# Two-pass attention and gated MLP on one core: another order of side work in slot one, in the pairs and at the end

## The chip, the core and the metric

One core of a Trainium2 chip runs the whole program. The metric is the device time of one launch in microseconds (us), the median of several runs. The engines are TensorE (PE, with its weight loads as PEld), VectorE (DVE), ScalarE (ACT), GpSimd (POOL) and SyncE (SP, which here only issues DMAs). Each runs its own list of instructions in order and waits where an input is not there yet.

## The reference

```python
def _attn_ref(q, k, v):              # (4, 12, 448, 64)
    scores = (1.0 / np.sqrt(q.shape[-1])) * np.matmul(q, k.transpose(0, 1, 3, 2))
    scores = np.where(mask, -1000000000.0, scores)      # causal
    attn = np.exp(scores - np.max(scores, axis=-1, keepdims=True))
    attn = attn / (np.sum(attn, axis=-1, keepdims=True) + 1e-09)
    return np.matmul(attn, v)

def _moe_ref(x, w_in, w_out):        # x: (1792, 768), w_in: (768, 2048), w_out: (2048, 768)
    h = x @ w_in
    g = h * np.cos(h)
    return g @ w_out
```

The attention's result, with its heads side by side, is `x`.

## The kernel before

**Numbers in halves.** Every large product is made from upper and lower halves: a value `t` is cast to a short float (`hi`), and `lo` is what is left, `t - hi`. A product is then three matmuls, hi·hi, hi·lo and lo·hi. A *half* below is one such operation: the upper one is a cast on ACT (lines 590, 681, 958), the lower one a subtraction, mostly on POOL (591, 682, 961), in two places on DVE.

**Attention** (to about 185 us) makes `x` for all 1792 rows and keeps it on the chip. The MLP then runs in two passes over the rows.

**Pass one** takes the first 1024 rows in two blocks of 512 and walks through `w_in` and `w_out` in eight groups; a block in a group is a *slot*, 16 in all. In a slot, PE makes two sums of `x @ w_in` (`m1_sum`, lines 564 to 566, 36 matmuls) and then four *chunks* of `g @ w_out` for the slot before (`m2a_chunk`, line 660, 12 matmuls of 384 columns each); DVE takes each chunk out of the banks into `acc` (lines 646, 648). Chunks use two pairs of banks in turn, so the third chunk waits for DVE's add of the first. Beside this, `cosine_stages` (572 on ACT, 574 on DVE, 576 and 577 on ACT, 579 on DVE) makes `g` from each sum, and the next group's weights are prepared: `mask_stages` (157, 159, 161 on ACT), `pack_stages` (three DVE passes 168, 172, 176), `halve` (681 and 682, then DMAs to DRAM), and sums of weights (`first_side`, `total`, line 700 on POOL; `side_out` then takes their halves). Slot 0 has only its chunks' inputs from the attention; slot 1 is the first that prepares weights, and for it the old code shares the order of all others, with `ia`, `ib` the weights packed in this slot and `ic` the next one's.

**Pass two** takes the other 768 rows with Strassen-like sums: for each pair of groups seven products `product(nx, n)` (line 1003, nine matmuls) of block sums of `w_in` and `x`, from which `g`'s four blocks a11, a12, a21, a22 come, and seven block products `blocks(g, n)` (line 1023, nine matmuls) with `w_out`. One iteration of the loop `for g in range(NG - 1)` is called a *pair* here: it has seven *steps* of one product for the next pair and one block product for this one. In between stand, in the code's order: the cosine's passes (`begin`, `go`, `end`), the sums s1 to s4 of blocks of `g` (`less`, line 954 on POOL) and their halves (`hi` line 958, `lo` line 961), and the four sums of raw `w_out` blocks for the next pair (`sub(nx, i)` with i = 4, 5, 3, 6, line 954; their halves `w_hi`, `w_lo`). The raw weights of a pair come with one DMA (`load_raw`, line 951) into one buffer, so its load waits for the last `sub` of the pair before:

```python
sub(nx, 4)
if g:
    a21 = end("21")
go("12")
w_hi(nx, 4)
go("12")
```

**The end.** Seven accumulators of block products are merged into four by sums on POOL and DVE (`merge`, line 1034, three operations each), the last group's products are added by PE (`m2_part`, line 1041) and DVE subtracts these (`m2_out`, line 1051) and stores the rows (line 1052). In the order of the queues nothing is scheduled by a planner: the instructions stand on each engine as the code is written.

Of the kernel before, what the change touches and what calls it, by code (L numbers as in the profile page):

```python
# [21 lines left out]
def kernel(  # L22
# [15 lines left out]
    nc = tc.nc  # L38
# [571 lines left out]
    def mask(i):  # L610
        if i < len(todo):
            for masks[i] in mask_stages(staged[i], i == 1):
                yield
# [18 lines left out]
    def moe(ring, early, firsts):  # L632
        pend = None
        with tc.tile_pool(name="mo", bufs=1) as mo:
# [219 lines left out]
            def slot(g, t0, n, k, prev, first):  # L854
# [6 lines left out]
                if k > 1:  # L861
                    mb = mask(ib)
                    some(mb, 2)
                else:
                    mb = opening[1]
# [99 lines left out]
            def sub(g, i):  # L965
                if g >= NG - 1:
                    return
                w11, w12, w21, w22 = raws[min(g, 1)]
                t = mo.tile([P, EH], F32, tag="tr", bufs=3, name="tr")
                if i == 4:  # L970
                    less(t, w12, w11)
                elif i == 5:
                    less(t, w22, sums_of.pop(4)[0])
                elif i == 3:
                    less(t, w21, sums_of[5, 0])
                else:
                    less(t, w22, w12)
                w = wouts[g, i]
                sums_of[i] = t, (w[:, 0], w[:, 1])
                if i == 5:  # L980
                    sums_of[5, 0] = t
                return
# [64 lines left out]
            def m2_out(j, c, o, rows):  # L1047
                i = (TA + j * TH) // P + c
                for e in range(2):
                    d = part(rows[e], c)  # L1050
                    nc.vector.tensor_tensor(d, d, o[:, e, 0:EH], op=ALU.subtract)
                    nc.sync.dma_start(
                        out=out[i * P : (i + 1) * P, e * EH : (e + 1) * EH], in_=d
                    )
# [46 lines left out]
            for g in range(NG - 1):  # L1101
# [8 lines left out]
                sub(nx, 4)  # L1110
# [3 lines left out]
                w_hi(nx, 4)  # L1114
# [7 lines left out]
                blocks(g, 0)  # L1122
                a12 = end("12")
# [5 lines left out]
                w_lo(nx, 4, nc.vector)  # L1129
# [4 lines left out]
                sub(nx, 5)  # L1134
                lo(g_ops[6], s3)
                lo(g_ops[1], a12)
                w_hi(nx, 5)
# [3 lines left out]
                blocks(g, 2)  # L1141
                s4 = less(sm0, a12, s2)
                sub(nx, 3)
                hi(g_ops[2], s4)
                lo(g_ops[2], s4)
                w_hi(nx, 3)
# [6 lines left out]
                begin("22", o)  # L1153
                blocks(g, 3)
                w_lo(nx, 3, nc.vector)
                go("22")
                go("22")
                sub(nx, 6)
                w_lo(nx, 5)
                w_hi(nx, 6)  # L1160
                if last:
                    merge(5, 0, nc.gpsimd)
                fetch_in(4)
                if g + 2 < NG - 1:
                    load_raw(g + 2)
# [3 lines left out]
                blocks(g, 4)  # L1169
                a22 = end("22")  # L1170
                go("11")
                go("11")
                hi(g_ops[3], a22)
                w_lo(nx, 6)
                lo(g_ops[3], a22)
                if last:
                    merge(6, 5, nc.gpsimd)
# [4 lines left out]
                blocks(g, 5)  # L1182
                a11 = end("11")
                go("21")
                go("21")
                hi(g_ops[0], a11)
                lo(g_ops[0], a11)
                fetch_in(6)
                if last:
                    blocks(g, 6)  # L1190
                    r = end("21")
                    hi(g_ops[6], r)
                    lo(g_ops[6], r)
# [6 lines left out]
            merge(3, 6, nc.gpsimd)  # L1200
# [3 lines left out]
            merge(4, 6, nc.vector, (0,))  # L1204
            r = end("12")
            merge(4, 6, nc.vector, (1, 2))
            hi(g_ops[1], r)
            lo(g_ops[1], r)
# [85 lines left out]
```

## Time and profile before

| | |
|---|---|
| time, median of 3 runs | 642.78 us (642.08 to 643.11) |
| the profiled execution | 640.33 us |
| its span | 638.6 us |
| PE busy | 621.9 us, 97% of the span |
| DVE, ACT, POOL busy | 487.3, 427.5, 429.6 us |

The span runs from the first to the last instruction of the profiled execution; its time also holds what lies around it. Busy time is the sum of an engine's instructions. PE at 97% still has idle places, and where the granted clock is under 1.00 it is busy at a lower speed. A list of waits says for each engine and line what it waited for: microseconds in total, times, and the longest. The chain of waits is followed back from the last instruction.

### The profile page before, as it was taken

What the parts mean: (1) busy time and instruction counts of PE and PEld (TensorE: products, weight loads), DVE (VectorE), ACT (ScalarE), POOL (GpSimd) and SP (SyncE); (2) the same over time, 40 slices, a digit from 0 to 9 for tenths busy, and PEclk for the clock granted to TensorE, in tenths of its full rate; (3) what the DMA queues carried; (4) which work ended last, traced back from release to release, by engine and by line L of the source; (5) the groups of instructions that cost most, each with busy time, mean ns of one, the idle gap of its engine ahead of it and who ended that gap; (6) DMA issues with size and microseconds to landing.
All of it is one profiled execution on the core that took longest, in us unless ns stands there. A gap on an engine that the chain in (4) does not pass through costs nothing.

```text
span 638.6 us, 11491 instructions
## 1 busy us (share of the span) xinstructions
PE 621.9 (97%) x3709; PEld 545.0 (85%) x3709; DVE 487.3 (76%) x1085; ACT 427.5 (67%) x953; POOL 429.6 (67%) x423
## 2 busy tenths in 40 slices
PE   8999999999998999999999999999979999999996
PEld 6667776766677999999999999999979999999995
DVE  5888888888737777887787777734349878888887
ACT  6989998998866777787777777732335444644540
POOL 3666656666626878777877787743385797679664
PEclk9999999999999999999999999999979999999999
DMA  5546556556505887869786978589956647558204
GB/s 124 138 115 148 145 119 159 142 131 162 156 10 199 251 314 240 312 201 341 231 314 198 350 244 311 195 326 393 410 193 241 232 136 276 206 204 280 54 1 149
DMA packets 124988, 133.29 MB, mean 209 GB/s; under 512 B 73056, under 2 KB 109264, under 8 KB 124928
## 3 DMA queue, kind: packets, MB, share of 16 engines
q1 hardware_dynamic: 118112, 107.31, 53.1%
q0 software_dynamic: 4928, 24.78, 10.4%
q10 hardware_dynamic: 1888, 0.46, 0.3%
q8 instruction: 30, 0.49, 0.3%
q14 instruction: 30, 0.25, 0.1%
HBM read 82.58 MB, written 49.94 MB: 208 GB/s over the span
## 4 chain that ended last, share of the span: by engine, by line
PE 86%; DVE 7%; ACT 3%; issue 2%; POOL 1%; DVEq 0%; ACTq 0%; POOLq 0%
PE banks L660 20%; PE banks L1023 12%; PE banks L1003 11%; PE banks L441 7%; PE banks L565 6%; PE banks L566 6%; PE banks L564 6%; PE banks L346 5%; PE banks L417 4%; PE banks L355 3%; PE banks L319 2%; DVE pb L363 2%; PE banks L924 1%; PE banks L427 1%; PE banks L1041 1%
## 5 line engine op out<-in xcount | busy, mean ns | idle before, releaser
L648 DVE TENSOR_TENSOR acc<-acc,banks 128x768 f32<-128x768 f32 (+1 forms) x122 | 111.9, 931 | 46.0 <-PE banks L660 36.9
L660 PE MATMUL banks<-w,gh 128*128 128x384 f32 x512 | 109.8, 335 | 2.7 <-DVE acc L646 2.7
L395 POOL TENSOR_TENSOR pb<-pb,stat 128x768 f32<-128x768 f32 (+2 forms) x72 | 73.9, 1040 | 41.8 <-ACT flat L329 19.9
L660 PEld LDWEIGHTS banks<-w,gh 128*128 128x128 f32 x512 | 90.8, 188 | 4.4 <-DVE acc L646 3.1
L377 ACT ACTIVATE pb<-pb,stat 128x384 f32<-128x384 f32 (+1 forms) x144 | 72.5, 512 | 15.9 <-DVE stat L363 15.9
L564 PE MATMUL banks<-xa,w 128*128 128x512 f32 x192 | 75.0, 391 | 0.0
L566 PE MATMUL banks<-xa,w 128*128 128x512 f32 x192 | 75.0, 391 | 0.0
L565 PE MATMUL banks<-xa,w 128*128 128x512 f32 x192 | 75.0, 390 | 0.0
L660 PE MATMUL banks<-w,gl 128*128 128x384 f32 x256 | 65.1, 335 | 0.0
L363 DVE CUSTOM_DVE_ANT_0 pb<-banks,mask 128x384 f32<-128x384 f32 (+1 forms) x144 | 52.9, 418 | 15.6 <-PE banks L346 15.6
L682 POOL TENSOR_TENSOR w<-ct,w 128x768 fp32r<-128x768 f32 x28 | 51.8, 1851 | 13.4 <-DVE r L574 7.0
L591 POOL TENSOR_TENSOR gl<-r,gh 128x512 fp32r<-128x512 f32 x32 | 41.4, 1294 | 21.0 <-ACT gh L590 18.9
L576 ACT ACTIVATE r<-r 128x512 f32<-128x512 f32 (+1 forms) x56 | 32.8, 586 | 31.1 <-DVE r L574 30.8
L572 ACT ACTIVATE ni<-banks 128x512 int32<-128x512 f32 (+1 forms) x64 | 34.4, 537 | 28.6 <-PE banks L566 17.2
L574 DVE SCALAR_TENSOR_TENSOR r<-ni,banks 128x512 f32<-128x512 int32 (+1 forms) x56 | 35.0, 626 | 23.5 <-ACT ni L572 22.6
L441 PE MATMUL banks<-pm,vn 128*64 128x448 f32 (+3 forms) x384 | 46.8, 386 | 0.3
L660 PEld LDWEIGHTS banks<-w,gl 128*128 128x128 f32 x256 | 46.4, 188 | 0.0
L441 PEld LDWEIGHTS banks<-pm,vn 128*64 128x64 f32 x384 | 25.5, 136 | 23.2 <-issue 13.3
L1003 PE MATMUL banks<-xb,bb 128*128 128x384 f32 x234 | 44.7, 334 | 0.0
L579 DVE SCALAR_TENSOR_TENSOR r<-r,banks 128x512 f32<-128x512 f32 (+1 forms) x56 | 35.0, 625 | 12.4 <-ACT r L577 12.4
L1023 PE MATMUL banks<-big,gh 128*128 128x384 f32 x168 | 42.7, 335 | 0.1
L566 PEld LDWEIGHTS banks<-xa,w 128*128 128x128 f32 x192 | 36.0, 188 | 7.6
(148 smaller groups left out, 1562.0 us busy)
## 6 DMA issues: line engine op xcount, KB each, us to landing
bb<-w_in_d SPq DMA_DIRECT2D x48, 384.0 KB, 5.5
land<-in_moe_w_in_dram SPq DMA_DIRECT2D x14, 768.0 KB, 5.3
land<-in_moe_w_out_dram SPq DMA_DIRECT2D x14, 768.0 KB, 5.7
w_out_d<-w POOLq DMA_DIRECT2D x14, 768.0 KB, 5.6
big<-w_out_d SPq DMA_DIRECT2D x25, 384.0 KB, 3.9
w_in_d<-w POOLq DMA_DIRECT2D x7, 768.0 KB, 3.8
raw_d<-ct POOLq DMA_DIRECT2D x14, 384.0 KB, 6.3
w_in_d<-str SPq DMA_DIRECT2D x27, 192.0 KB, 3.2
```

Source lines behind the costliest of these rows:

```text
L363: nc.vector.tensor_tensor_reduce(out=dst, in0=src, in1=m, scale=-1.0, scalar=3.0e38, op0=ALU.add, op1=ALU.min, accum_out=st[:, 0, n : n + 1],)
L377: nc.scalar.activation(dst, dst, AF.Exp, scale=-1.0, bias=st[:, 0, n : n + 1], accum_out=st[:, 1, n : n + 1],)
L395: nc.gpsimd.tensor_tensor(dst, dst, r.to_broadcast(list(dst.shape)), op=ALU.mult)
L441: nc.tensor.matmul(o[heads(j), kc * P : S], lhsT=vn[:, kc, heads(j)], rhs=pm[:, kc, j, kc * P : S], start=(kc == 0), stop=(kc == NB),)
L564: yield nc.tensor.matmul(hv, lhsT=wh[:, f], rhs=x[:, 0, cc, t], start=(cc == 0), stop=False)
L565: yield nc.tensor.matmul(hv, lhsT=wh[:, f], rhs=x[:, 1, cc, t], start=False, stop=False)
L566: yield nc.tensor.matmul(hv, lhsT=wl[:, f], rhs=x[:, 0, cc, t], start=False, stop=(cc == NCC - 1))
L648: nc.vector.tensor_tensor(d, d, o, op=ALU.subtract)
L660: nc.tensor.matmul(o[:, e, 0:EH], lhsT=a[:, cs], rhs=w[:, e * EH : (e + 1) * EH], start=(x == 0), stop=(x == 5),)
L682: nc.gpsimd.tensor_tensor(w[:, 1], tf, f32(w[:, 0]), op=ALU.subtract)
L1003: nc.tensor.matmul(o, lhsT=w[:, u, k * P : (k + 1) * P], rhs=x[k][:, v], start=k + m == 0, stop=k == K - 1 and m == 2,)
L1023: nc.tensor.matmul(o[:, b % 2, 0:EH], lhsT=g_ops[i][u][:, c * P : (c + 1) * P], rhs=wouts[g, i][:, v], start=(x == 0), stop=(x == 2),)
```

## The change

Three places of the order are written anew; what is computed stays the same.

**Slot one of pass one** (`k == 1`) gets an order of its own. One pack stands ahead of the cosine of the second sum, and the second pack, with its halves, behind the first chunk. **In each pair**, `sub(nx, 4)` and its halves move two steps later, `sub(nx, 5)` and `sub(nx, 3)` one, `sub(nx, 6)` one; `load_raw` two; the lower half of weight sum 3 goes from DVE to POOL, and DVE's lower half of weight sum 4 now stands ahead of `blocks(g, 3)`; the halves of a22 and a11 stand ahead of the cosine's passes. **In the last pair and the end** POOL's merges stand a step earlier, `merge(4, 6)` behind `end("12")`, a21's halves ahead of a11's lower half, and six of twelve stores are issued on ACT.

```diff
                 run(m1_sum(ring, g, 0, t0, n, hv[0]))
...
+                if k == 1:
+                    c0 = cosine_stages(hv[0], n)
+                    some(c0, 3)
+                    run(pack(ia, mo))
+                    some(firsts)
+                    some(opening[1])
+                    (r0,) = c0
+                    ta = halve(ia)
+                    gs.append(split(r0, *g_tiles(n)))
+                    run(m1_sum(ring, g, 1, t0, n, hv[1]))
+                    c1 = cosine_stages(hv[1], n)
+                    some(c1, 2)
+                    m2a_chunk(*prev, 0)
+                    pb = pack(ib, mo)
+                    some(pb)
+                    some(c1)
+                    m2a_chunk(*prev, 1)
+                    run(pb)
+                    tb = halve(ib)
+                    (r1,) = c1
+                    gs.append(split(r1, *g_tiles(n)))
+                    first_side(1, ta, tb)
+                    run(mask(ic))
+                    m2a_chunk(*prev, 2)
+                    m2a_chunk(*prev, 3)
+                    side_out()
+                    store_side()
+                    return gs
...
-                    nc.sync.dma_start(
+                    (nc.sync, nc.scalar)[e].dma_start(
...
-                sub(nx, 4)
                 if g:
                     a21 = end("21")
                 go("12")
-                w_hi(nx, 4)
                 go("12")
...
                 hi(g_ops[1], a12)
-                w_lo(nx, 4, nc.vector)
...
-                sub(nx, 5)
                 lo(g_ops[6], s3)
                 lo(g_ops[1], a12)
-                w_hi(nx, 5)
+                sub(nx, 4)
...
                 s4 = less(sm0, a12, s2)
-                sub(nx, 3)
                 hi(g_ops[2], s4)
+                w_hi(nx, 4)
                 lo(g_ops[2], s4)
-                w_hi(nx, 3)
+                sub(nx, 5)
...
                 begin("22", o)
+                w_lo(nx, 4, nc.vector)
                 blocks(g, 3)
-                w_lo(nx, 3, nc.vector)
+
+                if last:
+                    merge(5, 0, nc.gpsimd)
+                    merge(6, 5, nc.gpsimd)
                 go("22")
                 go("22")
-                sub(nx, 6)
+                w_hi(nx, 5)
+                sub(nx, 3)
                 w_lo(nx, 5)
-                w_hi(nx, 6)
-                if last:
-                    merge(5, 0, nc.gpsimd)
                 fetch_in(4)
-                if g + 2 < NG - 1:
-                    load_raw(g + 2)
...
                 a22 = end("22")
+                hi(g_ops[3], a22)
                 go("11")
                 go("11")
-                hi(g_ops[3], a22)
-                w_lo(nx, 6)
+                w_hi(nx, 3)
                 lo(g_ops[3], a22)
                 if last:
-                    merge(6, 5, nc.gpsimd)
+                    merge(3, 6, nc.gpsimd)
+                sub(nx, 6)
+                w_lo(nx, 3)
...
                 a11 = end("11")
+                hi(g_ops[0], a11)
                 go("21")
                 go("21")
-                hi(g_ops[0], a11)
-                lo(g_ops[0], a11)
+                w_hi(nx, 6)
+                if not last:
+                    lo(g_ops[0], a11)
+                w_lo(nx, 6)
                 fetch_in(6)
+                if g + 2 < NG - 1:
+                    load_raw(g + 2)
                 if last:
                     blocks(g, 6)
-                    r = end("21")
-                    hi(g_ops[6], r)
-                    lo(g_ops[6], r)
+                    a21 = end("21")
+                    hi(g_ops[6], a21)
+                    lo(g_ops[6], a21)
+                    lo(g_ops[0], a11)
...
-            merge(3, 6, nc.gpsimd)
             go("12")
             go("12")
             merge(5, 4, nc.vector)
-            merge(4, 6, nc.vector, (0,))
-            r = end("12")
-            merge(4, 6, nc.vector, (1, 2))
-            hi(g_ops[1], r)
-            lo(g_ops[1], r)
+            a12 = end("12")
+            hi(g_ops[1], a12)
+            lo(g_ops[1], a12)
+            merge(4, 6, nc.vector)
             merge(1, 0, nc.gpsimd)
```

How the instructions then stand, at three places. First DVE in slot one of pass one, from the attention's last operation (line 461) on; `ct` is a pack's result, `r` a cosine's, `acc` a chunk's sum:

```order
-L168 SCALAR_TENSOR_TENSOR banks<-land,banks 128x2x384
-L172 SCALAR_TENSOR_TENSOR banks<-land,banks 128x2x384
-L176 SCALAR_TENSOR_TENSOR ct<-land,banks 128x768
-L574 SCALAR_TENSOR_TENSOR r<-ni,banks 128x512
-L168 SCALAR_TENSOR_TENSOR banks<-land,banks 128x2x384
-L172 SCALAR_TENSOR_TENSOR banks<-land,banks 128x2x384
-L579 SCALAR_TENSOR_TENSOR r<-r,banks 128x512
-L176 SCALAR_TENSOR_TENSOR ct<-land,banks 128x768
+L574 SCALAR_TENSOR_TENSOR r<-ni,banks 128x512
+L168 SCALAR_TENSOR_TENSOR banks<-land,banks 128x2x384
+L172 SCALAR_TENSOR_TENSOR banks<-land,banks 128x2x384
+L176 SCALAR_TENSOR_TENSOR ct<-land,banks 128x768
+L579 SCALAR_TENSOR_TENSOR r<-r,banks 128x512
 L574 SCALAR_TENSOR_TENSOR r<-ni,banks 128x512
 L646 TENSOR_SCALAR acc<-banks 128x768
-L579 SCALAR_TENSOR_TENSOR r<-r,banks 128x512
-L646 TENSOR_SCALAR acc<-banks 128x768 x3
+L168 SCALAR_TENSOR_TENSOR banks<-land,banks 128x2x384
+L646 TENSOR_SCALAR acc<-banks 128x768
+L172 SCALAR_TENSOR_TENSOR banks<-land,banks 128x2x384
+L176 SCALAR_TENSOR_TENSOR ct<-land,banks 128x768
+L579 SCALAR_TENSOR_TENSOR r<-r,banks 128x512
+L646 TENSOR_SCALAR acc<-banks 128x768 x2
```

The first chunk's add stood behind two packs; now one pack stands ahead of it, and the second is spread behind it.

Second POOL at the start of the first pair of pass two; `tr<-raw` is `sub(nx, 4)`, the three rows `cs` and `sm` are s1, s2, s3, rows that end in `big` or `gh` are lower halves. Before:

```order
L961 TENSOR_TENSOR gl<-r,gh 128x384 x2
L954 TENSOR_TENSOR tr<-raw 128x384
L954 TENSOR_TENSOR cs<-r 128x384
L954 TENSOR_TENSOR cs<-cs,r 128x384
L954 TENSOR_TENSOR sm_4789<-r 128x384
L961 TENSOR_TENSOR big<-cs,big 128x384 x2
L954 TENSOR_TENSOR tr<-raw,tr 128x384
L961 TENSOR_TENSOR big<-sm_4789,big 128x384
L961 TENSOR_TENSOR gl<-cs,gh 128x384
L954 TENSOR_TENSOR cs<-cs 128x384
```

And of the change:

```order
L986 TENSOR_TENSOR gl<-r,gh 128x384 x2
L979 TENSOR_TENSOR cs<-r 128x384
L979 TENSOR_TENSOR cs<-cs,r 128x384
L979 TENSOR_TENSOR sm_4789<-r 128x384
L986 TENSOR_TENSOR big<-cs,big 128x384 x2
L986 TENSOR_TENSOR big<-sm_4789,big 128x384
L986 TENSOR_TENSOR gl<-cs,gh 128x384
L979 TENSOR_TENSOR tr<-raw 128x384
L979 TENSOR_TENSOR cs<-cs 128x384
```

The raw weights' sum stood ahead of s1; now s1, s2, s3 and four halves stand ahead of it, and s4 (`cs<-cs`) behind it.

Third DVE at the end, from the last pair's cosine on; rows with line 1034 (1056) are merges, those with 1051 (1073) the last subtractions. Before:

```order
L574 SCALAR_TENSOR_TENSOR cs<-ni,banks 128x384
L1034 TENSOR_TENSOR acc<-acc 128x384 x4
L579 SCALAR_TENSOR_TENSOR cs<-cs,banks 128x384
L1034 TENSOR_TENSOR acc<-acc 128x384 x2
L1051 TENSOR_TENSOR acc<-acc,banks 128x384 x6
```

And of the change:

```order
L574 SCALAR_TENSOR_TENSOR cs<-ni,banks 128x384
L1056 TENSOR_TENSOR acc<-acc 128x384 x3
L579 SCALAR_TENSOR_TENSOR cs<-cs,banks 128x384
L1056 TENSOR_TENSOR acc<-acc 128x384 x3
L1073 TENSOR_TENSOR acc<-acc,banks 128x384 x6
```

One merge has moved from ahead of the cosine's last pass to behind it.

## Rows read from the trace of the kernel before

**Rows 1.** Page, busy time by engine: us, share of the span, instructions.

```profile
PE 621.9 (97%) x3709; PEld 545.0 (85%) x3709; DVE 487.3 (76%) x1085; ACT 427.5 (67%) x953; POOL 429.6 (67%) x423
```

**Rows 2.** Waits of PE: line, releaser, us in total, times, longest.

```profile
PE banks L1023 <- DVE acc L646: 4.3, 1, 4.3
PE banks L660 <- DVE acc L646: 2.7, 1, 2.7
```

**Rows 3.** Timeline, first pair: start, us, instruction, [idle before, releaser].

```profile
464.52 1.01 POOL L954 TENSOR_TENSOR tr<-raw 128x384 f32<-128x384 f32 x1 [4.83 <-DMA raw<-raw_d]
...
467.56 1.38 DVE L961 TENSOR_TENSOR big<-tr,big 128x384 fp32r<-128x384 f32 x1
```

**Rows 4.** Chain of waits, first pair, groups of nine: start, us, what.

```profile
470.42 3.22 PE banks L1023 x9
473.64 2.75 PE banks L1003 x9
...
477.96 1.56 PE banks L1003 x9
```

**Rows 5.** Windows: PE, PEld, DVE, ACT, POOL busy, granted clock, DMA share, GB/s.

```profile
470.42:476.39 5.97, 5.97 (x19) 5.97 (x20) 2.14 (x3) 1.54 (x3) 5.97 (x7) 0.52 0.06 22
```

**Rows 6.** Later pairs: chain, timelines of DVE and PE, durations of line 961.

```profile
598.52 1.80 PE banks L1023 x9
...
587.02 1.81 DVE L648 TENSOR_TENSOR acc<-acc,banks 128x768 f32<-128x768 f32 x2
...
589.00 1.20 PE L1023 MATMUL banks<-big 128*128 128x384 f32 x6
...
L961 DVE TENSOR_TENSOR big<-tr,big x12: 551/1316/1435, 467.6 to 588.7; 128x384 fp32r<-128x384 f32 x12
```

**Rows 7.** Chain of waits in slot one, to the third chunk.

```profile
198.81 0.95 DVE ct L176
199.75 0.60 DVE r L574
200.35 0.88 DVE acc L646
201.27 4.56 PE banks L660 x24
```

**Rows 8.** Timeline of ACT in slot one.

```profile
194.38 0.82 ACT L161 ACTIVATE banks<-flat 128x768 f32<-128x768 f32 x1 [3.60 <-DVE ct L176]
195.13 0.58 ACT L572 ACTIVATE ni<-banks 128x512 int32<-128x512 f32 x1
195.61 0.83 ACT L681 CAST w<-ct 128x768 fp32r<-128x768 f32 x1
...
198.92 0.62 ACT L590 CAST gh<-r 128x512 fp32r<-128x512 f32 x1 [0.67 <-DVE r L579]
```

**Rows 9.** Timelines of POOL, ACT and DVE, slot one's tail and slot two.

```profile
200.87 1.82 POOL L682 TENSOR_TENSOR w<-ct,w 128x768 fp32r<-128x768 f32 x1
...
206.06 0.51 ACT L590 CAST sst<-str 128x384 fp32r<-128x384 f32 x1 [1.17 <-POOL str L700]
...
209.78 0.82 ACT L161 ACTIVATE banks<-flat 128x768 f32<-128x768 f32 x1 [1.32 <-DVE ct L176]
...
216.18 0.96 DVE L646 TENSOR_SCALAR acc<-banks 128x768 f32<-128x768 f32 x1 [0.36 <-PE banks L660]
```

**Rows 10.** The end: timelines of PE and DVE, durations (ns, min/median/max) of merges.

```profile
619.27 0.93 PE L1041 MATMUL banks<-big,gh 128*128 128x384 f32 x4
...
621.22 4.74 DVE L1034 TENSOR_TENSOR acc<-acc 128x384 f32<-128x384 f32 x4
...
632.29 2.86 DVE L1051 TENSOR_TENSOR acc<-acc,banks 128x384 f32<-128x384 f32 x6
...
L1034 DVE TENSOR_TENSOR acc<-acc x9: 544/870/1372, 621.2 to 631.8; 128x384 f32<-128x384 f32 x9
```

**Rows 11.** Line 951's six loads of raw weights, issue to landing.

```profile
DMA to landing us min/median/max: 4.2/4.4/8.6
```

More of the change, by code (lines that the diff above doesn't have):

```diff
@@ L860, in slot @@
                 run(m1_sum(ring, g, 0, t0, n, hv[0]))
[L861 to L865, printed above, removed]
+                if k == 1:
[26 more added lines that the diff above has]
+                    return gs
+                mb = mask(ib)
+                some(mb, 2)
                 run(pack(ia, mo))
@@ L972, in sub @@
                 elif i == 5:
-                    less(t, w22, sums_of.pop(4)[0])
+                    less(t, w22, sums_of[4][0])
                 elif i == 3:
-                    less(t, w21, sums_of[5, 0])
+                    less(t, w21, sums_of[5][0])
                 else:
@@ L979, in sub @@
                 sums_of[i] = t, (w[:, 0], w[:, 1])
-                if i == 5:
-                    sums_of[5, 0] = t
-                return
             def w_hi(g, i):
```

## The prediction

> **What bounds the kernel now.** I read the page first: TensorE (PE) is busy for 621.9 of 638.6 us [rows 1], so only PE's idle time, and work at a lowered clock, can be won. The list of what PE waits for has one long wait in pass two (4.3 us, once) and one in pass one (2.7 us, once), both for DVE's sums out of the banks [rows 2]. Each lies in a stretch that the change rewrites; the last twelve microseconds are the third place.
>
> **First pair of pass two: a gain of 7.2.** The timeline tells why PE stood [rows 3]. POOL, first in its queue, wanted the raw weights (`sub(nx, 4)`, line 954) and idled 4.83 us until their load had landed, at 464.52. Behind it in the same queue stood s1 and s2, whose halves PE's third group reads. ACT's and DVE's halves of the same weight sum stand early in their queues too: DVE's (1.38 us, at 467.56) stands ahead of the add of product 1, and so ahead of the sums that free PE's banks. Two engines are stopped by work that is wanted a whole pair later. After the wait PE works slowly: its next two groups take 3.22 and 2.75 us in place of 1.56 [rows 4], and the stretch has a granted clock of 0.52, the 1.2 GHz level [rows 5]. The engine had stood for 4.3 us before. The price is 4.3 + (3.22 - 1.56) + (2.75 - 1.56) = 7.2 us.
>
> The change puts s1, s2 and s3 first and `sub(nx, 4)` behind the third group's start. The inputs of s1 and s2 are complete when POOL is through with the lower half of a11, at 464.52 - 4.83 = 459.7. Five POOL operations of 1.0 us (s1, s2, s3, two halves, as the row at 464.52) end at 464.7. The halves that the third group reads are the first of the two, done a microsecond sooner, and two groups have to run on PE before they are read: without its stall PE gets there at 470.4 - 4.3 = 466. The margin is 2 us. The raw weights then wait for nobody: POOL comes to them two operations later, at 466.7, and they landed at 464.5. I take the whole 7.2. The lower bound is half of it (rival C).
>
> **The other pairs: a loss of 0.3.** Six pairs have weight sums. POOL gets one half more (`w_lo(nx, 3)`, 1.0 us, six times), hidden because POOL is idle for a third of the span [rows 1]; without that cover the lower half of a11, which PE wants at the start of the next pair, would be late. That half is late already: three pairs show a first group of 1.80 in place of 1.56 [rows 6]. ACT's upper half of a11 is now taken ahead of two cosine passes, so I count 3 x 0.24 = 0.7 as won. What is lost: DVE's half of weight sum 4 now stands in front of the two adds of the fourth group. Today these begin at 587.02, the first is through at 587.97, and PE's next group begins at 589.00 [rows 6]: a margin of 1.0 us. The DVE copy takes 0.55 us alone and up to 1.44 [rows 6], so PE loses 0 to 0.4 us a pair, 0 to 2.4 in six. POOL is at that moment between two halves, and the copy is long or short by a tenth of a microsecond's difference; I take 1.0. Net: +0.3.
>
> The long copies are those that met a POOL operation: the median is 1.32 against 0.55 alone [rows 6]. The Trainium skill ("SBUF — State Buffer", Who interferes with whom) says that a VectorE instruction with two SBUF inputs and a GpSimd instruction that reads SBUF exclude each other for a whole instruction, the later one being blocked. It speaks against this edit, and the trace agrees as far as these durations go.
>
> **Slot one of pass one: a gain of 2.0, and 2.4 lost in slot two.** PE's third chunk waits for DVE's add of the first chunk. That add ran at 200.35, behind both packs and the second `574`, and PE went on at 201.27 [rows 7]. Now one pack stands ahead of it. The first pack ended at 194.38 [rows 8]; one DVE operation (0.60) goes in front of it, so 194.95. From there ACT runs its mask copy 0.82, the upper halves 0.83, the cast 0.62 and the second cosine's first pass 0.58 [rows 8], then DVE 0.60 and the add 0.9 [rows 7]: 194.95 + 2.85 + 1.5 = 199.3. PE goes on at 199.3: 2.0 won, some 0.7 of the wait left.
>
> But the second pack has moved behind that add. DVE still has three pack passes (0.95) and one add (0.88) to do [rows 7]: 199.3 + 3.7 = 203.0, where it ended at 199.76. ACT's halves (0.83) end at 203.8. In the old order it took from 200.87, when POOL began these halves, to 206.06 until ACT could take the first sum of slot one's tail [rows 9], 5.2 us; now that is at 209.0. PE's third and fourth chunk took 4.56 us [rows 7], so PE entered slot two at 205.8 and does now at 203.9. ACT comes to slot two's work 5.1 us after PE, where it was 0.2: 4.9 later. Two cushions: ACT waited 1.32 us for DVE at 209.78, and the first chunk's add began at 216.18 and ended 0.95 later, at 217.1, where PE needed it at 218.2 (a chunk is 12 matmuls of 1.56/9, 2.1 us; the first ended at 216.1 and the second at 218.2) [rows 9, 4]. PE waits 4.9 - 1.3 - 1.1 = 2.5 us in slot two, less 0.1 for what the lesser stall of slot one spares. Net of the slots: +0.4. The bounds are -2.0 (slot two hides it all) and +1.5 (a further chunk waits too).
>
> **The end: a gain of 1.7.** DVE's last operations begin at 632.29 and last 2.86: 635.15 [rows 10]. Its nine merges took 0.54 us to 1.37 [rows 10]; the first four alone held DVE for 4.74 us, since POOL merged beside them, and the last pair's cosine and PE's last operand stood behind. Now POOL does its nine earlier merges a step sooner, three merges stand ahead of the cosine on DVE, not four, and most of them run alone. PE's 72 last matmuls, from 619.27, end at 619.27 + 72 x 1.56/9 = 631.8 if nothing stops them; two subtractions of 2.86/6 follow: 632.8, a gain of 2.4. With two of DVE's merges blocked (0.85 each, the third hidden) I reach 633.5, a gain of 1.7; 1.0 is the low end. Six of the twelve stores move to ACT's queue, which has nothing else to do then: costed at nothing, since the last store waits for the last subtraction in either queue.
>
> **Sum:** -7.2 + 0.3 + 0.4 - 1.7 = -8.2 us. The profiled execution took 640.33 us, its span 638.6; the median of the runs is 642.78, 2.45 higher. Taken from the median: 634.6 us.
>
> **Rivals.**
> (B) Slot two hides the lateness. For it: both cushions may be larger than the rows show, since ACT's order there lets passes slide. Against: 4.9 us is twice what the two rows give. Then 2.4 less: 632.2.
> (C) The first pair finds a new wait. POOL's s4 and the copies of weight sum 4 on ACT and DVE now stand behind the raw load, ahead of the fourth group's adds. If that load lands 4 us later, with other loads in front, PE waits some 3.6 there: 638.2. Against: at 464.5 it was in time by 2 us.
> (D) Every DVE copy of weight sum 4 meets POOL: 0.4 in all six pairs, 2.4 in place of 1.0, so 636.0. By the Trainium skill's page named above this is so whenever POOL is in an operation at that moment.
> (E) Slower: the raw load becomes the bound of every pair. On SP it moves behind two loads of `w_in` sums, which no longer wait behind it. It is now issued after `sub(nx, 6)` one step later and read two steps later, some 10 us after its issue (three and a third steps of 3.12). It lands after 4.2 to 8.6 us [rows 11]. Past some 11 us, PE would wait in five pairs, behind POOL, ACT's and DVE's copies and the fourth group's adds; it must take 13 us for 1.9 a pair, 9.5 in all: 644.1. The slowest row stands 4 us from that.
> (F) The waits only move, and the sum is nothing: 642.8.
>
> **Chances.** Forecast 0.50, B 0.18, C 0.14, D 0.10, E 0.04, F 0.04. A measurement of this kernel can tell about 0.2% from no change (1.3 us). Faster by more: A to D, 0.92; within: F, 0.04; slower: E, 0.04. The range reaches from B with the tail's better end and no copy blocked (632.2 - 0.7 - 1.0, and 0.3 for the runs' own spread) to C with the tail's lower end (638.2 + 0.7 + 0.3): 630.2 to 639.2.
>
> **What will show it.** Right: no PE wait for L646 near 466, no stretch at a clock of 0.5 in pass two, a slot one shorter by 2 us with a new PE wait of about 2.5 us in slot two, the fourth group's adds now and then late by a few tenths, and a last DVE operation about 1.7 us sooner against PE's start of the last stage. Wrong: a POOL wait for `raw` in later pairs, a PE wait at the third or fourth group of the first pair, or slot two without a wait.

## The result, and the profile after the change

The changed kernel took 632.27 us (median of 4 runs, 631.69 to 633.05), the kernel before 642.94 us beside it (4 runs, 642.08 to 643.29): a ratio of 0.9837, with a 95% interval of 0.982 to 0.9854. Such ratios and intervals come from the single runs and can differ a little from the quotient of the medians. The medians lie 10.67 us apart, the two profiled executions 8.6 (640.33 and 631.69), their spans 8.7. The forecast was 634.6, in a range of 630.2 to 639.2.

The page has PE busy for 618.8 us, 3.1 less than in [rows 1], and POOL busier by 5.6.

```profile
PE 618.8 (98%) x3709; PEld 542.7 (86%) x3709; DVE 479.5 (76%) x1079; ACT 427.9 (68%) x953; POOL 435.2 (69%) x429
```

The list of PE's waits holds no line of pass two any more; what [rows 2] showed there is gone, and the one line of pass one is three waits now, 0.5 us more in all.

```profile
PE banks L660 <- DVE acc L646: 3.2, 3, 2.3
```

Where these three lie is in PE's timeline of slots one and two (start, duration, instruction, idle time before it and its releaser). The first row is slot one's first chunk, the second its third chunk, which [rows 7] had at 201.27; the other two are the third and fourth chunk of slot two, which had no wait before.

```profile
194.40 0.87 PE L660 MATMUL banks<-w,gh 128*128 128x384 f32 x4
...
199.50 0.98 PE L660 MATMUL banks<-w,gh 128*128 128x384 f32 x4 [0.75 <-DVE acc L646]
...
218.61 0.96 PE L660 MATMUL banks<-w,gh 128*128 128x384 f32 x4 [2.26 <-DVE acc L646]
...
221.21 0.97 PE L660 MATMUL banks<-w,gh 128*128 128x384 f32 x4 [0.22 <-DVE acc L646]
```

In the first pair of pass two the chain of waits now runs without a break at 1.56 us a group of nine matmuls, where [rows 4] had 3.22 and 2.75:

```profile
465.71 1.56 PE banks L1025 x9
467.27 1.56 PE banks L1045 x9
468.83 1.56 PE banks L1025 x9
470.39 1.56 PE banks L1045 x9
```

POOL's timeline there answers to [rows 3]. s1 starts at 460.85 and the halves that PE's third group reads at 463.88; the raw weights come at 467.78 and nothing is waited for. PE reaches that group at 467.27.

```profile
460.85 1.01 POOL L979 TENSOR_TENSOR cs<-r 128x384 f32<-128x384 f32 x1
...
463.88 2.00 POOL L986 TENSOR_TENSOR big<-cs,big 128x384 fp32r<-128x384 f32 x2
...
467.78 1.02 POOL L979 TENSOR_TENSOR tr<-raw 128x384 f32<-128x384 f32 x1
```

DVE's six lower halves of weight sum 4 (`w_lo(nx, 4)`, a subtraction with both inputs in SBUF, called DVE's copy below; line 986, which was 961 in [rows 6]; min/median/max in ns) are all short, and the six raw loads land as in [rows 11], the slowest half a microsecond later:

```profile
L986 DVE TENSOR_TENSOR big<-tr,big x6: 548/580/600, 471.4 to 580.6; 128x384 fp32r<-128x384 f32 x6
...
DMA to landing us min/median/max: 4.1/4.2/9.1
```

At the end, beside [rows 10], PE's last stage begins at 612.59, DVE's merges (line 1056) come as three, three and three, and the last subtractions begin at 623.66 and end at 626.52. Before, PE itself stood in this stage for the last pair's cosine, which DVE had behind four merges; after, it does not, and its last two matmuls start 12.21 us into the stage in place of 13.29. The first row is of the kernel before.

```profile
626.47 0.79 PE L1041 MATMUL banks<-big,gh 128*128 128x384 f32 x3 [0.54 <-DVE cs L579]
```

```profile
612.59 0.93 PE L1063 MATMUL banks<-big,gh 128*128 128x384 f32 x4
...
614.53 2.32 DVE L1056 TENSOR_TENSOR acc<-acc 128x384 f32<-128x384 f32 x3
...
623.66 2.86 DVE L1073 TENSOR_TENSOR acc<-acc,banks 128x384 f32<-128x384 f32 x6
```

To say where the time went I cut both traces at the same places of the program: the first matmul of slot one's chunks (194.18 in the trace before, 194.40 after), the first matmul of pass two (437.33 and 438.51), the first of the last stage (619.27 and 612.59), the end of DVE's last row (635.15 and 626.52), and the span's end.

| stretch | before | after | difference | forecast |
|---|---|---|---|---|
| up to slot one's first chunk | 194.18 | 194.40 | +0.22 | none |
| slot one to pass two | 243.15 | 244.11 | +0.96 | +0.4 |
| pass two to the last stage | 181.94 | 174.08 | -7.86 | -6.9 |
| last stage to DVE's end | 15.88 | 13.93 | -1.95 | -1.7 |
| DVE's end to the span's end | 3.45 | 3.38 | -0.07 | 0 |
| sum | 638.6 | 629.9 | -8.7 | -8.2 |

So the gain comes from pass two and the end, and the edit of slot one costs a microsecond. The first row, and the gap between profiled executions and medians, are for the experiments.

### The profile page after: what moved, and what is told of

It is laid out like the page before. It is cut to its first block, busy times and chain, and to the rows that moved or that the text cites. A ratio compares the mean times of both kernels' runs of the same rounds, so it can differ in the third digit from the quotient of the medians.

```text
span 629.9 us, 11493 instructions
## 1 busy us (share of the span) xinstructions
PE 618.8 (98%) x3709; PEld 542.7 (86%) x3709; DVE 479.5 (76%) x1079; ACT 427.9 (68%) x953; POOL 435.2 (69%) x429
## 4 chain that ended last, share of the span: by engine, by line
PE 88%; DVE 6%; ACT 3%; POOL 1%; issue 1%; DVEq 0%; ACTq 0%
PE banks L660 19%; PE banks L1045 12%; PE banks L1025 12%; PE banks L441 7%; PE banks L565 6%; PE banks L566 6%; PE banks L564 6%; PE banks L346 5%; PE banks L417 4%; PE banks L355 3%; PE banks L319 3%; PE banks L949 2%; PE banks L1063 2%; DVE pb L363 2%; PE banks L427 1%
```

## The experiments

### Each part by itself

**First pair alone.** The kernel before, with its first pair in the new order and the six others in the old one:

```diff
+                if g == 0:
+                    if g:
+                        a21 = end("21")
...
+                else:
+                    sub(nx, 4)
...
```

> The kernel before with the new order in the first pair of pass two alone. Theory (raw load held POOL's first subtraction, and with it ACT, DVE and PE): the 4.3 us stall and the half clock behind it go, 7.2 us less than before, and the spans of slots and end stay as they were. Rival (the transfer itself bounds the pair, or the stall moves to a later raw sum): under 3 us less, with a new wait on POOL or PE inside this pair.

Measured: 635.45 us against 642.01, a ratio of 0.9894 (0.9873 to 0.9914), so 5.5 to 8.2 us less. In its trace pass two takes 175.87 us up to the last stage, 6.07 less than before. The stall of 4.3 and the slow groups are gone; two small waits that the kernel before did not have stand in this pair and in the next:

```profile
474.20 1.85 PE L1020 MATMUL banks<-big 128*128 128x384 f32 x9 [0.20 <-DVE acc L646]
...
490.31 1.80 PE L1020 MATMUL banks<-big 128*128 128x384 f32 x9 [0.21 <-DVE acc L648]
```

The first stands behind a DVE copy of weight sum 4 that took 1.42 us (at 471.86) where the changed kernel's took 0.55. PE's next group begins 1.69 us later, so this wait costs some half a microsecond: 0.20 idle, 0.16 of overlap between groups that is lost, 0.13 in a slower group. The second, worth as much, comes from joining two orders: the new first pair issues the next raw load later than the old second pair wants it, and POOL waits 0.65 us for it (at 484.35). With both added, the stall was worth about 7 us, as the theory has it.

**Last pair and end alone.** The kernel before, with the new order where `last` holds, the new final merges, and the stores on two queues:

```diff
+                if last:
+                    if g:
+                        a21 = end("21")
...
+                else:
+                    sub(nx, 4)
...
-            merge(3, 6, nc.gpsimd)
...
-            merge(4, 6, nc.vector, (0,))
-            r = end("12")
-            merge(4, 6, nc.vector, (1, 2))
+            a12 = end("12")
...
+            merge(4, 6, nc.vector)
...
-                    nc.sync.dma_start(
+                    (nc.sync, nc.scalar)[e].dma_start(
```

> The kernel before with the new order of the last pair, the final merges and the stores on two queues alone. Theory: DVE ends 2.0 us sooner behind the start of TensorE's last stage, 2.0 us less than before. Rival (the stores on ACT's queue are what saves, and DVE's order is hidden by them): DVE ends as before, and the time from DVE's end to the span's end falls by over 1 us.

Measured: 640.42 us against 642.01, 0.9976 (0.996 to 0.9992). From the last stage's start to DVE's end it is 13.91 us, 1.97 less than before and as in the changed kernel; from there to the span's end 3.41 (3.45 before). The rival falls: the order of the merges pays, the second queue of stores does not show. How much is POOL's and how much DVE's part of that order was not tested; of the 1.97, 1.08 is PE's, whose last two matmuls start 12.21 us into the stage here too.

This trace has the old first pair, and the stall is the same, 4.21 us, but of the two groups behind it only one is slow; the granted clock over both (472.38 to 477.22) is 0.67, where [rows 5] had 0.52:

```profile
472.38 3.22 PE banks L1020 x9
475.60 1.62 PE banks L1000 x9
```

By the working of the prediction the stall cost 5.9 us here, where it was 7.2 in the kernel before and 7.0 in slot one alone. So its idle time stays between 4.2 and 4.3 us, and what is lost behind it varies by over a microsecond.

**Slot one alone, and all but slot one.** The kernel before with the new branch `if k == 1`, and the changed kernel without it:

```diff
-                if k == 1:
-                    c0 = cosine_stages(hv[0], n)
...
-                    store_side()
-                    return gs
-                mb = mask(ib)
-                some(mb, 2)
+                if k > 1:
+                    mb = mask(ib)
+                    some(mb, 2)
+                else:
+                    mb = opening[1]
```

> The kernel before with the new order of slot one of pass one alone. Theory: TensorE's wait in slot one falls from 2.7 to 0.7 us and a wait of about 2.3 us comes in slot two; 0.5 to 1.2 us more than before. Rival (the wait in slot two has another cause, and slot one's gain stands): 2.0 us less than before.

> The changed kernel with slot one in the order of before. Theory: 0.5 to 1.2 us less than the changed kernel, so about 631.4 us, with TensorE's single wait of 2.7 us in slot one and none in slot two. Rival (slot one's edit pays): 2 us more than the changed kernel, 634.3 us.

Measured: slot one alone 642.89 us against 642.01, 1.0011 (0.9998 to 1.0023): not the gain of 2 that the rival wanted. All but slot one: 632.57 us, 0.9842 (0.982 to 0.9865), which the times can't tell from the changed kernel's 0.9837. The traces can. From slot one's first chunk to pass two it is 243.13 us with the old slot one (243.15 in the kernel before) and 244.11 with the new one. In slot one alone it is 244.56, 1.41 more than before where the theory had 1.2 at most; 0.43 of that is lost in slot three, where PE's timeline lists no wait. The waits of both kernels stand there as the theory had them: 0.74, 2.31 and 0.22 in slot one alone, and in the kernel without the new slot one:

```profile
201.21 0.97 PE L660 MATMUL banks<-w,gh 128*128 128x384 f32 x4 [2.75 <-DVE acc L646]
```

### The same 2.7 us wait, with and without a fall of the clock

The profiled execution of the first pair alone should have had the slot one of before, yet its stretch from slot one to pass two took 244.60 us in place of 243.15; that of the end alone took 244.60 too. Their orders there are the kernel before's, and so are their waits (2.74 and 2.75 us). The chain of waits has the 24 matmuls behind the wait at 6.00 us, where [rows 7] had 4.56; the window over them (PE, PEld, DVE, ACT, POOL busy, granted clock, DMA share, GB/s), first of the kernel before, then of the first pair alone:

```profile
201.27:205.83 4.56, 4.56 (x25) 4.41 (x26) 2.51 (x3) 3.60 (x5) 4.23 (x4) 1.00 0.87 305
```

```profile
201.50:207.50 6.00, 6.00 (x25) 6.00 (x26) 2.51 (x3) 4.81 (x7) 5.59 (x6) 0.72 0.65 231
```

After the same idle time PE went on at 2.4 GHz in the one execution and partly at 1.2 GHz in the other. Over all traces of this study, the wait of 2.7 us of the old slot one was followed by a lowered clock in two of four, and that of 2.3 us in the new slot two in three of six (it costs 1.45 us behind the old wait, 1.09 behind the new one). Waits of 4.2 to 4.3 us in pass two, and of 3.2 (in two parts) and 3.5 in the two kernels of the next section, were followed by one each time; no wait of up to 1.14 us in these two slots was. Where such a fall comes or not, executions of one kernel differ by over a microsecond. The timed runs have no traces, but each has its mean granted clock. Of the changed kernel's five runs in the second comparison (further down) the one at 1.000 took 632.51 us, the four at 0.995 or 0.996 took 633.72 to 634.43; of all but slot one the run at 0.999 took 630.41, the three at 0.995 or 0.996 took 632.48 to 632.78. The four runs of the result were at 0.998 to 1.000, so part of their low median is luck of the clock. In the kernel before the tie is weaker: nine runs at 0.990 took 642.03 to 645.11, the 32 others 640.68 to 643.59. What else makes the medians differ 2 us more than the two profiled executions is not shown.

### Which queue stopped PE in the first pair

Two kernels put back what stood early in the first pair, one engine at a time: POOL's sum alone, then POOL's sum and ACT's copy (its upper half, `w_hi`). The edit of the second is shown; the first has not the lines around `w_hi`.

```diff
+                if not g:
+                    sub(nx, 4)
                 if g:
                     a21 = end("21")
                 go("12")
+                if not g:
+                    w_hi(nx, 4)
                 go("12")
...
-                sub(nx, 4)
+                if g:
+                    sub(nx, 4)
...
-                w_hi(nx, 4)
+                if g:
+                    w_hi(nx, 4)
```

> The changed kernel with POOL's sum for operand 4 back at the head of the first pair, its copies on ACT and DVE left late. Theory (POOL's own queue is enough to stop TensorE): the sum waits for its load to about 465.7 us, the low half of the third group's sum comes at about 470.7 us, and TensorE, due at 467.3, waits 3.4 us there, released by POOL and no longer by DVE's add; 3.4 to 5 us more than the changed kernel, by what the clock does behind it. Rival (it was ACT and DVE, held behind the copies, that stopped TensorE): no wait over 0.5 us in this pair, time as the changed kernel.

> The same with ACT's copy of that sum back in its old place too, and DVE's copy late. Theory: ACT goes on at about 466.7 us and its cosine steps hold DVE's adds, but these then come at about the time of POOL's low half, so the wait stays near 3.4 us; only DVE's copy in its old place, 1.38 us long in the kernel before, makes it 4.3. Rival (each queue adds its own delay): a wait of 4.3 us or more.

Measured: 638.89 us with POOL's sum alone and 638.30 with ACT's copy too, against 641.79 (0.9955, 0.9941 to 0.997; 0.9941, 0.9925 to 0.9957). Pass two takes 179.64 and 179.15 us up to the last stage, 5.56 and 5.07 more than in the changed kernel. With POOL's sum alone, PE's third group is held first by the upper half, which ACT could make only from POOL's late sum, and then by POOL's lower half, 3.15 us together:

```profile
472.52 0.62 PE L1045 MATMUL banks<-big 128*128 128x384 f32 x2 [2.40 <-ACT big L983]
473.89 2.61 PE L1045 MATMUL banks<-big 128*128 128x384 f32 x7 [0.75 <-POOL big L986]
```

```profile
468.88 1.01 POOL L979 TENSOR_TENSOR tr<-raw 128x384 f32<-128x384 f32 x1 [5.16 <-DMA raw<-raw_d]
```

With ACT's copy early as well, the wait is one of 3.50 us:

```profile
473.05 3.12 PE L1045 MATMUL banks<-big 128*128 128x384 f32 x9 [3.50 <-ACT big L983]
```

So POOL's queue, stopped by the load, is enough for about three quarters of the stall of 4.33, and ACT's copy adds 0.35. That DVE's copy brings the other 0.8 follows by difference only; no kernel put it back. Both rivals fall: ACT and DVE alone did not do it, and two early queues give less than 4.3 us. The theory missed two things: PE is released first by ACT's half, which waits for POOL, where it had POOL's own half, and the loss is larger than its 3.4 to 5 us in the first kernel, since the groups behind the wait are slow here too (2.61 us for seven matmuls).

### Whether DVE's copy of weight sum 4 costs anything

```diff
                 plus(u2, o, u2)
+                w_lo(nx, 4, nc.vector)
                 plus(o, o, u3)
                 begin("22", o)
-                w_lo(nx, 4, nc.vector)
                 blocks(g, 3)
```

It ran beside the changed kernel itself:

> The changed kernel itself once more, as the measure for the three kernels that run beside it. Both theories: 0.9837 of the kernel before, 0.3% either way, with 3.2 us of waits in slots one and two.

> The changed kernel with DVE's copy of operand 4 one instruction earlier in each pair, ahead of the second addition to the fourth group's bank. Theory (a copy that comes while POOL is within an instruction waits for its end; in the changed kernel it starts just at that end): the copies last 1.0 to 1.4 us in place of 0.58, each pair's adds come that much later, and TensorE loses about 0.5 us a pair, some 3 us over the six pairs. Rival (DVE's copy has room to spare in each pair): the copies lengthen or not, TensorE does not wait, time as the changed kernel.

Measured: the changed kernel 633.73 us against 642.48, 0.9859 (0.9834 to 0.9884); with the copy earlier 633.51, 0.9857 (0.9833 to 0.988): the rival's time, not the theory's 3 us more. The copies do last longer, all six:

```profile
L986 DVE TENSOR_TENSOR big<-tr,big x6: 916/1004/1008, 472.4 to 582.0; 128x384 fp32r<-128x384 f32 x6
```

In the first of them the copy starts while POOL is in an instruction, and lasts until 0.41 us after that one's end (472.87); POOL's next two then take 2.43 us in place of about 2.0:

```profile
472.36 0.92 DVE L986 TENSOR_TENSOR big<-tr,big 128x384 fp32r<-128x384 f32 x1
```

```profile
471.85 1.02 POOL L986 TENSOR_TENSOR gl<-cs,gh 128x384 fp32r<-128x384 f32 x1 [0.62 <-ACT gh L983]
472.82 2.43 POOL L979 TENSOR_TENSOR tr<-raw,tr 128x384 f32<-128x384 f32 x2
```

The Trainium skill ("SBUF — State Buffer", Who interferes with whom) says that a VectorE instruction with two SBUF inputs contends with a GpSimd instruction that reads SBUF, that the port pair they share is an exclusive lock, and that the order of issue decides who blocks. These rows agree, in both directions: here the copy lasts 0.92, and POOL's two 2.43. But of the price of 0.5 us a pair that the theory put on it little is left: pass two is longer by 0.48 us in all, in groups of 1.63 to 1.66 us in place of 1.56. In the changed kernel the first pair's copy begins 0.01 us behind a POOL instruction and takes 0.55, while POOL's two take 2.53:

```profile
471.36 2.53 POOL L979 TENSOR_TENSOR tr<-raw,tr 128x384 f32<-128x384 f32 x2
```

```profile
471.37 0.55 DVE L986 TENSOR_TENSOR big<-tr,big 128x384 fp32r<-128x384 f32 x1
```

In three other executions with this order in the first pair (first pair alone, and the two kernels of the next section that ran first) it begins 0.01 or 0.02 us behind POOL's start as well, and it is the copy that waits. Pass two is then half a microsecond longer (174.57 in place of 174.08). From the second of those two kernels:

```profile
471.24 2.30 POOL L980 TENSOR_TENSOR tr<-raw,tr 128x384 f32<-128x384 f32 x2
```

```profile
471.26 1.42 DVE L987 TENSOR_TENSOR big<-tr,big 128x384 fp32r<-128x384 f32 x1
```

So the copy stands on an edge, as the prediction said, where the rows hardly tell the two cases apart; but only in the first pair, and there in three of seven executions with this order, does it fall on the dear side.

### Why slot two is late, and a faster kernel

In the changed kernel ACT stands still in slot one's tail for POOL's first sum, ahead of the masks of slot two:

```profile
209.22 0.52 ACT L590 CAST sst<-str 128x384 fp32r<-128x384 f32 x1 [2.09 <-POOL str L700]
209.64 1.00 ACT L157 ACTIVATE flat<-land,flat 128x768 f32<-128x768 f32 x1
...
212.40 0.58 ACT L572 ACTIVATE ni<-banks 128x512 int32<-128x512 f32 x1
```

The copy that waits there (line 590, of `side_out`) is needed by nobody in that slot. Four kernels take it out:

```diff
                     m2a_chunk(*prev, 3)
-                    side_out()
-                    store_side()
                     return gs
```

The first two have this, and the second the order of adds besides. In both, slot three writes a sum's tile again before its lower half has been stored, so that this part of what is computed differs.

> The changed kernel with the copy and store of the first sum taken out of the end of slot one (slots two and three take it in with their own). Theory (ACT, waiting 2.1 us for that sum of POOL, is what makes slot two late): ACT's mask of slot two starts some 2 us earlier, TensorE's wait in slot two falls from 2.26 to about 0.75 us, and the time is 1.0 to 1.7 us less than the changed kernel's. Rival (POOL's later work or DVE's packs make slot two late): the wait stays over 1.8 us, time within 0.4 us of the changed kernel's.

> The same, and in slot two the first chunk's matmuls and its add placed ahead of the second cosine's first two steps on ACT and DVE. Theory: DVE's add comes 0.7 us earlier than in the kernel above and the wait of slot two goes to 0.2 us or less: 1.5 to 2.2 us less than the changed kernel's. Rival (the second cosine, pushed back, makes slot three late): no better than the kernel above, with a new wait in slot two or three.

Measured: 632.20 us (0.9841, 0.9825 to 0.9857) and 631.51 (0.9839, 0.9826 to 0.9853), against 641.79. The waits in the two slots fall to 0.74, 0.98 and 0.22 us in the first, where its theory had 0.75 for slot two, and the stretch from slot one to pass two takes 242.83 us, 1.28 less (1.0 to 1.7 forecast). In the second, slot two's third chunk waits 0.40 but its fourth 1.14: the second add still stands behind the second cosine's last step and comes 7.25 us after the slot's first matmul of a chunk, 6.92 in the first kernel. The stretch takes 243.17 us, so its rival was right. Their times alone do not tell them from the changed kernel, which did not run beside them.

The other two ran beside it, with a call of `store_side()` ahead of slot three's sums. The last of them has two more edits:

```diff
+                if k == 2:
+                    step(0)
                 some(c1, 2)
-                step(0)
+                if k == 2:
+                    step(1)
+                else:
+                    step(0)
...
                 go("22")
+                w_lo(nx, 4, nc.vector)
                 go("22")
```

> Slot one without the copy and store of the first sum at its end, all sums stored before their tiles are written again. Theory: waits in slots one and two 1.9 us in place of 3.2, and 1.3 us less than the changed kernel beside it. Rival (the sums that are carried on make slot three late): the waits come back in slot three, time within 0.4 us of the changed kernel.

> The same; in slot two the first two chunks' adds ahead of the second cosine's steps on DVE; and in each pair DVE's copy of operand 4 behind the 22 sum's first DVE step, where POOL is idle. Theory: the waits of both slots come to 1.2 us or less, no copy lasts over 0.7 us, and the time is 2.0 to 2.6 us less than the changed kernel's beside it. Rival (the second cosine or the 11 sum of each pair becomes late): a new wait in slot three or in the pairs, time as the kernel above or more.

Measured: 630.66 us (630.21 to 631.33, 5 runs; 0.9816, 0.9795 to 0.9837) and 630.93 (0.9824, 0.9799 to 0.985), where the changed kernel beside them took 633.73 (632.51 to 634.43, 5 runs). The first beats both kernels: none of its runs is as long as any of the changed kernel's. Its spans differ from that one's by 3.0 us in the profiled executions: 0.67 before slot one, and 2.35 from slot one to pass two (242.85 against 245.20). The changed kernel's first execution, without a fall of the clock there, took 244.11: measured against it 1.26 is the shorter waits, and the other 1.09 the clock, which fell behind the changed kernel's wait of 2.28 in this execution and not behind waits of up to 1.00. PE's timeline of the faster kernel:

```profile
199.74 0.96 PE L660 MATMUL banks<-w,gh 128*128 128x384 f32 x4 [0.74 <-DVE acc L646]
...
217.59 0.97 PE L660 MATMUL banks<-w,gh 128*128 128x384 f32 x4 [1.00 <-DVE acc L646]
...
220.19 0.96 PE L660 MATMUL banks<-w,gh 128*128 128x384 f32 x4 [0.24 <-DVE acc L646]
```

The last kernel cuts slot two's wait to 0.39 and holds all copies at 0.55 us, as its theory said, but two waits of 0.16 and 0.22 come in slot three, as its rival said, and 242.72 us in that stretch is as good as 242.85: no gain over the kernel above.

## Why the prediction was right, and where it was not

- **First pair, -7.2: right**, mechanism and size. POOL's wait for the raw load, with s1 and s2 behind it, was the cause; put back by itself it brings 3.15 us of wait and 5.56 us in all. The size belongs to the execution that it was read from: the same stall cost 5.9 and 7.0 us in two other traces with the old order, by how long the groups behind it stayed slow. What lay behind it then was as late as I said, and nothing else took its place: POOL's margin was 2.4 where I had 2 (the two halves begin at 463.88 with a microsecond each, and PE wants the first at 467.27).
- **Other pairs, +0.3: wrong in sign.** Pass two fell by 7.86, 0.7 beyond the first pair's 7.2. The three late groups of 1.80 [rows 6] are gone, as counted, but the reason given for them, ACT's upper half of a11 ahead of two cosine passes, was never tested by itself, and the traces point to another. (Of the halves of a22 and a11 only ACT's upper ones moved ahead of the passes.) In the old order DVE takes the lower half of weight sum 3 just ahead of the cosine's passes; the change gives it to POOL. Four traces have later pairs in the old order (before, first pair alone, end alone, slot one alone), 23 such halves together. Twelve took 1.30 us or more, and behind each of these a late group follows; eleven took 0.55 to 0.95, and none does. In the kernel before, the half in the row below is followed by a late group at 510.72 (1.78 us), and the next pair's, 0.60 us at 523.00, by none:

```profile
500.94 1.32 DVE L961 TENSOR_TENSOR big<-tr,big 128x384 fp32r<-128x384 f32 x1
```

In slot one alone one such half took 2.30 us (at 546.00), PE then waited 0.46 for POOL's lower half of a11, and the later pairs lost 1.8 us in place of 0.7. No kernel makes one of the two moves without the other. On the side of the losses, the step that failed is "I take 1.0" for DVE's copies ahead of the adds: it was 0 in this execution. The margin ahead of the adds was there in the rows; blocked copies (0.92 to 1.01 us) cost 0.10 a pair or less in the kernel that had them in all six, not the 0 to 0.4 between which I chose. Only the long copy of 1.42, in the first pair of three other executions, cost as much as the upper end and a tenth more (0.49).
- **Slots, +0.4: measured +0.96.** The times of the path were right to 0.2 us, with the later start of 0.22 still in them: PE on at 199.50 (199.3 forecast), the second pack's end at 203.03 (203.0), ACT at 209.22 (209.0), waits in slot two of 2.26 and 0.22 (2.5). The step that failed is "PE waits 4.9 - 1.3 - 1.1 = 2.5 us": the idle time came out, 2.48, but I priced a wait at its idle time alone. From the first chunk of slot two to its end PE took 8.35 us before (213.87 to 222.22) and 11.41 now (212.00 to 223.41): 3.06 more for 2.48 of idle time. A wait also ends the overlap of 0.17 between groups and the group behind it is 0.1 slower; two new waits make that 0.58. Where the clock falls behind the wait in slot two, as in three of six traces, it is 1.09 more.
- **End, -1.7: right**, -1.95, nearer the better bound; alone it gives -1.97. PE's last operand came from behind the merges, as I said: 1.08 of it is PE's. The stores on ACT's queue are worth nothing that shows, as costed.
- **Rivals.** B: slot two did not hide the lateness. C: no new wait behind the raw load. D: not in this kernel, and forced upon it it costs 0.5, not 2.4. E: the raw loads of the pairs land after 9.1 us at most, and POOL waits for none of them. F: a wait only moved in the slots, and nowhere else.
- **The number.** Spans and profiled executions fell by 8.7 and 8.6 where the sum had 8.2. That this is so close is in part luck: the pairs gave 1.0 more than forecast and the slots cost 0.56 more. The medians fell by 10.67 in the first comparison and by 8.75 in the second, which is nearer the sum and was measured with the clock down in four of five runs of the changed kernel; the forecast of 634.6 lies 2.3 above the first median and 0.9 above the second.

## What to carry to other kernels

A step that waits for a load must not stand in a queue ahead of work that has its data already: one weight sum and its two halves, moved behind the work of the moment on three engines, gave some 7 of the 9 us. Price a wait of PE at its idle time, plus some 0.3 us for the group behind it, plus the chance that the clock falls; so when a wait is only moved, as in slot one, two short ones are not cheaper than one of the same length. And look at what is at the end of a slot before moving its beginning: a copy that nobody there needed held ACT for 2.1 us. A half on DVE took 0.55 us or up to 2.3, by what POOL did beside it; ask what stands behind it before choosing the engine.

## What was not expected of the hardware

- The same wait is followed by a lower clock in some executions and not in others: after 2.7 us of idle PE the granted clock over the next 24 matmuls was 1.00 in the kernel before and 0.72 in the first pair alone, at a price of 1.45 us.
- Which of DVE's copy and POOL's instruction waits can turn within some hundredths of a microsecond, and the starts in the trace do not tell it: with the copy 0.01 us behind POOL's start DVE took 0.55 and POOL's two 2.53 in the changed kernel, and DVE 1.42 and POOL's two 2.30 in the first of the four kernels without the copy at the end of slot one. A half on DVE can also wait for two POOL instructions in a row: 2.30 us, in slot one alone.
- Slot one's first chunk began between 194.07 and 196.66 us in the fourteen traces, though no kernel changes what PE runs ahead of it. In nine of them PE waits 0.4 to 1.1 us for loads of `q`, in five it does not. The four kernels of one set, which ran on another chip than the two other sets, begin at 195.23 to 196.66, and of the ten others only one begins after 194.80, so the chip may have a part in it; that was not tested. The spread is larger than the gain of several of the edits, so spans were compared by stretches.
